# Loads of q in two parts, zeroing in smaller pieces, and two moved steps around the turn of chunk 5, in a retention and squared-ReLU kernel on one core

## The chip, the cores and the metric

The kernel runs on one core of one Trainium2 chip. Its time is the device time of one execution in microseconds (us). Before the change the median of three runs was 203.47 us (203.37, 203.47 and 203.81). A smaller number is better.

The engines are named as in the profile: PE is TensorE's matrix multiply and PEld its load of weights, DVE is VectorE, ACT is ScalarE, POOL is GpSimd, and SP is SyncE, which issues most DMAs. A suffix q (SPq, POOLq) marks work of an engine's queue, such as the issue of a DMA.

## The reference

```python
batch, n_heads, seq, head_dim = (4, 8, 768, 64)
gamma = 1.0 - 2.0 ** (-5.0 - np.arange(H))
for t in range(S):
    state = gamma[None, :, None, None] * state + einsum('bhd,bhe->bhde', k[:, :, t], v[:, :, t])
    y[:, :, t] = scale * einsum('bhd,bhde->bhe', q[:, :, t], state)
x = y.transpose(0, 2, 1, 3).reshape(3072, 512)
h = np.maximum(x @ w_in, 0.0)        # w_in: 512 x 2048
out = (h * h) @ w_out                # w_out: 2048 x 512
```

Inputs and output are float32; the output is 3072 x 512.

## The kernel before, in words

**Tiling.** The 3072 tokens are 24 chunks of 128 (six for each of the four batch entries). For a chunk the recurrence becomes matrix products: scores (k times q, masked), a state that is carried from chunk to chunk in PSUM, and outputs (values times masked scores, plus q times the state so far). The outputs of a chunk are the columns `xt` that the feed-forward part reads. That part works in blocks: block 0 has chunks 0 to 3, and each later block has two chunks. A block has a first product with `w_in`, a ReLU on ACT that moves it out of PSUM, a square on DVE, and a second product with `w_out`.

**Seven products.** For the last two chunks of block 0, and for the later blocks, the second product is not done plainly but by a scheme with seven half-size products in place of eight (in the manner of Strassen and Winograd). It needs sums of pieces of `h` made beforehand on DVE: `s1`, `s2` (`first_sums`), `s3` (`third_sums`, L1021) and `s4` (`fourth_sums`, L1025). It also needs differences of pieces of `w_out`, which `sum_w_out` (L338) makes in `w_sum`. For block 0 all this is `last_of_first` (L983). Its generator `second_products` (L1029) interleaves the plain second product of chunks 0 and 1, which collect in two PSUM tiles `ops`, with the seven products of chunks 2 and 3, in `pa`, `pb`, `pd` and `pe`. The last of the seven, which is the reader of `s4`, is kept back (`last_product`, L1091) and run inside block 1.

**Order.** Nothing is reordered by the compiler: each engine runs its instructions in the order in which the Python emits them, and waits by semaphores on the other engines. The order is written by hand. The feed-forward part is cut into numbered places, 8 for each chunk. `put(place, what, ...)` notes a step, and `before(n)` (L1370) emits all steps of place n, in the order in which they were put, between two pieces of the feed-forward part. The steps that were put by `ffn_pieces(0)`, which include the sums of `h`, are put when that generator starts, and so come last in their place. Block 0 covers the places up to 32, and block 1 begins behind place 32.

**The stretch around chunk 5.** `attend(5, None, (25, 27, 30, 32, 34))` (L1331) spreads chunk 5's steps. Place 25 has the scaling of k and the copy of v into `v_bd` on POOL (`scale_kv`, L397). Place 27 has its turn, `transpose_k` (L426): four transposes on PE into the PSUM tile `tp` and two copies on ACT (L437), one for each 64 rows of `k_bd`. Place 30 has the first half of the scores, place 32 the second half, and place 34 the outputs. `scores` (L448) has four products into the single buffer of `st` and one masking multiply on DVE (L463), which writes `pt`. The second half can start only when the mask of the first half has read `st`. `attend(6, 30, ...)` puts the two scalings of q of chunk 6 (`scale_q`, L391) at place 30, behind chunk 5's scores.

**Loads.** `load_q` (L88) brings the q of two chunks, eight heads, in one DMA of 512 KB on SP's queue, into one of two buffers. `load_kv` brings k or v of one chunk on SP. From chunk 8 on, k comes packed, by DMAs that POOL issues (`k_loads`), into `k_bigs`. The parts of `k_bigs` off the block diagonal are zeroed by POOL memsets at places 16, 34 and 43 and the ones behind them (L1341).

Of the kernel before, what the change touches and what calls it, by code (L numbers as in the profile page):

```python
# [31 lines left out]
def kernel(  # L32
# [14 lines left out]
    C = 128  # L47
# [37 lines left out]

    raw_q, raw_k, raw_v = {}, {}, {}

    def load_q(m):  # L88

        b, i = chunks[m]  # L90
        t = ldqpool.tile([P, H, 2, D], FP32, name="qn")
        src = q[b, :, i * C : (i + 2) * C, :].rearrange("h (s r) d -> s h r d", r=2)
        nc.sync.dma_start(t[:], src)
        raw_q[m] = t

    heads_of = [slice(0, H // 2), slice(H // 2, H)]
# [886 lines left out]
    def last_of_first():  # L983

        def halves_of(k, c):
            return [
                t.rearrange("e (j k) (c t) -> e k c j t", k=2, c=4)[:, k, 2 + c] for t in h2s[0]
            ]

        (a11, a12), (a21, a22) = ([halves_of(k, c) for k in range(2)] for c in range(2))  # L990
        n = NFB // 4
        s1, s2, s4 = (
            [
                t.rearrange("e (x j t) -> e x j t", x=2, t=C)[:, x]
                for x in range(2)
            ]
            for t in (spare[:, i * HN * 4 : (i + 1) * HN * 4] for i in range(3))
        )
        s3 = a21
        b = lambda k, c: lambda j: w_out_bf[j // 2][:, 2 * (j % 2) + k, c * HN : (c + 1) * HN]  # L1000
        t1, t2, t3, t4 = (lambda j, t=t: t[:, j] for t in sums)

        def add(out, in0, in1, op=ALU.add):
            nc.vector.tensor_tensor(out=out, in0=in0, in1=in1, op=op)

        def product(to, left, right, js, start=True, stop=True):
            for j in js:
                nc.tensor.matmul(  # L1008
                    to,
                    lhsT=left[j // n][:, j % n],  # L1010
                    rhs=right(j),
                    start=(start and j == 0),
                    stop=(stop and j == NFB // 2 - 1),
                    skip_group_check=True,
                )

        def first_sums(x):
            add(s1[x], a21[x], a22[x])
            add(s2[x], s1[x], a11[x], ALU.subtract)

        def third_sums():  # L1021
            for x in range(2):
                add(s3[x], a11[x], a21[x], ALU.subtract)

        def fourth_sums():  # L1025
            for x in range(2):
                add(s4[x], a12[x], s2[x], ALU.subtract)

        def second_products():  # L1029
            ops = [ps_f.tile([P, DM], FP32, name="psf") for _ in range(2)]  # L1030
            pa, pe, pd, pb = (
                t[:, n * HN : (n + 1) * HN]
                for t in [ps_f.tile([P, DM], FP32, name="psf") for _ in range(2)]
                for n in range(2)
            )
            oa, ob = (opool.tile([P, DM], FP32, name="osb") for _ in range(2))
            a, u, v = (upool.tile([P, HN], FP32, name=f"u{i}") for i in range(3))
            r0 = 2 * C

            def plain(j):  # L1040
                for f in (2 * j, 2 * j + 1):
                    for c, op in enumerate(ops):
                        nc.tensor.matmul(  # L1043
                            op[:],
                            lhsT=h_of(0, f)[:, 0, c * C : (c + 1) * C],
                            rhs=w_out_bf[f // FPQ][:, f % FPQ, :],
                            start=(f == 0),
                            stop=(f == NFB - 1),
                        )
                product(pa, a11, b(0, 0), (j,))  # L1050

            lo, hi = range(0, 4), range(4, 8)
            for j in range(4):
                plain(j)
                yield
            product(pd, s1, t1, lo)
            product(pb, s2, t2, lo, False)
            yield
            for j in range(4, 6):
                plain(j)  # L1060
                yield
            product(pe, a22, t4, lo, False)
            yield
            plain(6)
            yield
            plain(7)
            nc.scalar.activation(a[:], pa, AF.Copy)
            for c, op in enumerate(ops):
                osb = opool.tile([P, DM], FP32, name="osb")
                nc.scalar.activation(osb[:], op[:], AF.Copy)  # L1070
                nc.sync.dma_start(out[c * C : (c + 1) * C], osb[:])
            yield
            product(pd, s1, t1, hi)
            product(pb, s2, t2, hi)
            add(u[:], pb, a[:])
            yield
            product(pa, a12, b(1, 0), lo, False)
            yield
            product(pa, a12, b(1, 0), hi, False)
            nc.scalar.activation(oa[:, 0:HN], pa, AF.Copy)  # L1080
            yield
            product(pb, s3, t3, lo, False)
            yield
            product(pb, s3, t3, hi, False)
            add(v[:], pb, a[:])
            add(ob[:, HN:DM], pd, v[:])
            yield
            product(pe, a22, t4, hi)
            add(ob[:, 0:HN], pe, v[:])

            def last_product():  # L1091
                product(pd, s4, b(1, 1), range(8), False)
                add(oa[:, HN:DM], pd, u[:])
                yield
                nc.sync.dma_start(out[r0 + C : r0 + 2 * C], ob[:])
                yield
                nc.sync.dma_start(out[r0 : r0 + C], oa[:])
                yield

            kept.append(last_product())  # L1100
            yield

        return first_sums, (third_sums, fourth_sums), second_products
# [27 lines left out]
    def ffn_pieces(tb):  # L1131
        nch = BLOCKS[tb]
        TB = nch * C
        if tb == 0:
            first_sums, last_sums, second_products = last_of_first()
            put(11, first_sums, 0)
            put(17, first_sums, 1)
            put(26, last_sums[0])
            put(27, last_sums[1])
            for f in range(FPQ, NFB):  # L1140
                hp = ps_f.tile([P, TB], FP32, name="psf")
                first_product(tb, hp[:], f, slice(0, TB))
                relu(h_of(tb, f)[:, 0], hp)
                yield
            yield from second_products()
            return
        elif tb <= 2:

            for c in range(nch):
                for g in range(NQ):  # L1150
                    first_unit(tb, g, c)
                    if c * NQ + g in (1, 2, 3) and kept:
                        next(kept[0])
                    if c * NQ + g == 4:
                        kept.clear()
                    if tb in SEVEN and (c, g) == (1, 2):
                        first_sums, rest = seven_products(tb)
                        first_sums(slice(0, 4))
                    yield
            if tb in SEVEN:  # L1160
                yield from rest()
                return
        else:
            h_tiles(tb)
            per = 512 // TB
            if tb in SEVEN:
                first_sums, rest = seven_products(tb)
            for f0 in range(0, NFB, per):
                hp = ps_f.tile([P, per, TB], FP32, name="psf")
                for f in range(f0, f0 + per):  # L1170
                    first_product(tb, hp[:, f - f0, :], f, slice(0, TB))
                relu(h_of(tb, f0, f0 + per), hp, tb in SEVEN and f0 // per in (1, 3))
                if f0 // per in (1, 2, 3) and kept:
                    next(kept[0])
                if f0 // per == 4:
                    kept.clear()
                if f0 // per == 5 and tb in SEVEN:
                    first_sums(slice(0, 4))
                yield
            if tb in SEVEN:  # L1180
                yield from rest()
                return
# [102 lines left out]
    def put(place, what, *args):  # L1285
        parts.setdefault(place, []).append((what, args))
# [31 lines left out]
        put(place, load_w_out, g)  # L1318
    for m, which, place in ((4, "v", 10), (5, "k", 12), (5, "v", 14)):
        put(place, load_kv, m, which)  # L1320
    put(15, load_q, 6)
    for m, which, place in ((6, "k", 16), (6, "v", 17), (7, "k", 18), (7, "v", 19)):
        put(place, load_kv, m, which)
    put(10, cast_w, "in", 3)
# [15 lines left out]

    for j, t in enumerate(k_bigs):  # L1341
        for hh in range(2):
            put((16, 34, 43)[j] + hh, nc.gpsimd.memset, t[halves[hh], :, :, 1 - hh, :], 0.0)

    put(20, load_q, 8)
    put(41, load_q, 10)
    done = [57, 62] + [70 + 8 * j for j in range(14)]

    ahead = {
# [62 lines left out]
```

## Time and profile before

| What | Value |
|---|---|
| Median of three runs | 203.47 us |
| The profiled execution's own time | 203.39 us |
| Its span, first to last instruction | 201.6 us |
| PE busy | 195.0 us |
| DVE busy | 151.0 us |
| ACT busy | 127.1 us |
| POOL busy | 82.7 us |

The span is 1.8 us shorter than the execution's own time, which also holds what lies before the first and behind the last instruction. In rows of the timeline the first number is the start in us from the span's start, and the second is how long the row lasts. Then come the engine, the line of the kernel, the operation, what is written from what, the shape and the number of instructions put together in the row. In square brackets stands how long the engine was idle before the row and what ended that. A matmul is pipelined: the row's end is modelled and overlaps the next one, so PE's pace is read from start to start, not from the busy time.

### The profile page before, as it was taken

The page shows a single profiled execution, that of the slowest core. Times are in us where ns is not written, and L with a number is a line of the kernel's source. Part 1 is how long each engine was busy: PE and PEld are TensorE (multiplying, and loading weights), DVE is VectorE, ACT ScalarE, POOL GpSimd, SP SyncE. Part 2 cuts the span into 40 slices and gives each one's busy share as a digit, 9 for nine tenths or more (in the row PEclk, how much of TensorE's full clock was granted, in tenths as well). Part 3 has the DMA queues.
Part 4 walks back from the last instruction along what each step waited for, and adds up shares of the span by engine and source line. Part 5 has one row for each costly group of instructions (what it writes and reads, how often), then busy time and mean ns, then how long its engine had stood idle before and what let it go on. Part 6 is the DMA issues. An engine that isn't in the chain of part 4 may idle for free.

```text
span 201.6 us, 5846 instructions
## 1 busy us (share of the span) xinstructions
PE 195.0 (97%) x2362; PEld 164.6 (82%) x2362; DVE 151.0 (75%) x327; ACT 127.1 (63%) x258; POOL 82.7 (41%) x150
## 2 busy tenths in 40 slices
PE   7799999999999999999999999999999999999991
PEld 2468445779988999899999999999999999999881
DVE  3986899799598886777687697697696696484472
ACT  8864875264863666774766866864865865845710
POOL 8683760899930762154422185116362202200000
PEclk9999999999999999999999999999999999999999
DMA  5999999999987999599979399999999762101102
GB/s 166 356 375 397 343 192 196 252 201 227 305 174 182 176 163 238 172 134 180 189 152 206 114 170 221 158 242 141 192 153 140 197 94 67 66 0 52 55 0 106
DMA packets 92250, 36.02 MB, mean 179 GB/s; under 512 B 68544, under 2 KB 88256, under 8 KB 92224
## 3 DMA queue, kind: packets, MB, share of 16 engines
q1 hardware_dynamic: 73088, 31.47, 66.5%
q0 software_dynamic: 19136, 4.20, 23.3%
q8 instruction: 18, 0.29, 0.6%
q14 instruction: 8, 0.07, 0.1%
HBM read 27.26 MB, written 6.29 MB: 166 GB/s over the span
## 4 chain that ended last, share of the span: by engine, by line
PE 91%; DVE 4%; DMA 2%; issue 1%; ACT 0%; DVEq 0%
PE psf L847 42%; PE psf L884 21%; PE tp L884 7%; PE psf L1043 3%; PE psf L1008 2%; DMA qn<-in_q_dram 2%; PE y L804 2%; PE st L748 2%; PE y L797 2%; PE c_ps L775 2%; PE c_ps L653 1%; PE y L532 1%; PE st L456 1%; PE y L368 1%; DVE qs L559 1%; DVE osb L880 1%
## 5 line engine op out<-in xcount | busy, mean ns | idle before, releaser
L847 PE MATMUL psf<-xt,w_in_bf 128*128 128x256 bf16 (+2 forms) x864 | 92.3, 261 | 0.0
L847 PEld LDWEIGHTS <-w_in_bf 128*128 128x128 bf16 x864 | 70.8, 98 | 11.2
L856 ACT ACTIVATE h<-psf 128x512 bf16<-128x512 f32 x96 | 56.2, 594 | 24.3 <-PE psf L847 22.0
L726 POOL COPY v_bd<-v 64x512 bf16<-64x512 bf16 x32 | 21.7, 677 | 76.5 <-DVE v L718 75.6
L827 DVE TENSOR_TENSOR h<-h 128x512 bf16<-128x512 bf16 x80 | 32.8, 423 | 19.1 <-ACT h L856 18.4
L884 PEld LDWEIGHTS <-h 128*128 128x128 bf16 x344 | 31.7, 98 | 3.7 <-issue 0.2
L156 POOL DMA_DIRECT2D k_big<-in_k_dram x40 | 26.6, 686 | 0.1
L884 PE MATMUL psf<-w_sum,h 128*128 128x256 bf16 x168 | 23.5, 273 | 0.0
L884 PE MATMUL tp<-w_out_bf,h 128*128 128x256 bf16 x136 | 19.1, 273 | 0.0
L880 DVE TENSOR_TENSOR u<-psf,u 128x256 f32<-128x256 f32 x20 | 8.5, 424 | 12.7 <-PE psf L884 11.8
L884 PE MATMUL psf<-w_sum,k_bd 128*128 128x256 bf16 x144 | 17.9, 273 | 0.0
L880 DVE TENSOR_TENSOR osb<-psf,u 128x256 f32<-128x256 f32 x29 | 11.4, 420 | 6.6 <-PE psf L884 6.3
L884 PEld LDWEIGHTS <-k_bd 128*128 128x128 bf16 x144 | 13.8, 98 | 1.5
L784 ACT ACTIVATE s_bd<-c_ps 64x256 bf16<-64x256 f32 x29 | 10.7, 369 | 6.3 <-PE c_ps L775 6.3
L387 DVE TENSOR_TENSOR qs<-qn,qf 128x512 bf16<-128x512 f32 x20 | 13.7, 688 | 0.0
L785 ACT ACTIVATE s_bd<-c_ps 64x256 bf16<-64x256 f32 x29 | 11.0, 379 | 0.4
L755 DVE TENSOR_TENSOR pt<-st,cmask 128x512 bf16<-128x512 f32 x16 | 11.0, 687 | 0.2
L718 DVE TENSOR_TENSOR v<-stage,kf 128x512 bf16<-128x512 f32 x16 | 10.9, 683 | 0.0
L920 ACT ACTIVATE osb<-tp 128x256 f32<-128x256 f32 x8 | 3.1, 384 | 12.2 <-PE tp L884 12.2
L811 ACT ACTIVATE xt<-y 128x512 bf16<-128x512 f32 x16 | 9.6, 598 | 1.8 <-PE y L804 1.2
L825 ACT ACTIVATE h<-h 128x512 bf16<-128x512 bf16 x16 | 10.1, 630 | 0.5
L880 DVE TENSOR_TENSOR k_bd<-h 128x512 bf16<-128x512 bf16 x18 | 9.9, 553 | 0.3
(147 smaller groups left out, 290.1 us busy)
## 6 DMA issues: line engine op xcount, KB each, us to landing
qn<-in_q_dram SPq DMA_DIRECT2D x12, 512.0 KB, 5.7
out_dram<-osb SPq DMA_DIRECT2D x23, 256.0 KB, 2.6
stage<-in_v_dram SPq DMA_DIRECT2D x32, 96.0 KB, 3.9
stage<-in_moe_w_in_dram SPq DMA_DIRECT2D x4, 512.0 KB, 6.8
stage<-in_moe_w_in_dram SPq DMA_DIRECT2D x2, 1024.0 KB, 10.7
w_out_bf<-in_moe_w_out_dram POOLq DMA_DIRECT2D x4, 512.0 KB, 10.4
kn<-in_k_dram SPq DMA_DIRECT2D x6, 256.0 KB, 6.2
k_big<-in_k_dram POOLq DMA_DIRECT2D x32, 48.0 KB, 3.8
```

The lines of the kernel that those rows point to most:

```text
L156: nc.gpsimd.dma_start(t[rows, 2 * at_w : 2 * (at_w + size), p, hh, :], half_rows(k, b, 2 * p + hh, i + w, size),)
L387: engine.tensor_tensor(out=out, in0=by, in1=table[:, :, None].to_broadcast([P, H, D]), op=ALU.mult)
L718: nc.vector.tensor_tensor(out=v2.rearrange("s (u p) d -> s u p d", u=2), in0=vn, in1=kf2[:, i, :, :, None].to_broadcast([P, 2, NPAIR, D]), ...
L726: nc.gpsimd.tensor_copy(v_bd[rows, :, hh, :], v2[rows])
L755: nc.vector.tensor_tensor(out=pt[:], in0=st[:], in1=cmask2.rearrange("s r t -> s (r t)")[:, None, :].to_broadcast([P, 2 * NPAIR, C // 2]), ...
L784: nc.scalar.activation(s_bd[halves[0], :, 0, :], c[halves[0]], AF.Copy)
L785: nc.scalar.activation(s_bd[halves[1], :, 1, :], c[halves[1]], AF.Copy)
L827: nc.vector.tensor_mul(hv, hv, hv)
L847: nc.tensor.matmul(hp, lhsT=w_in_bf[g][:, cb, fq * 128 : (fq + 1) * 128], rhs=xts[tb][:, cb, cols], start=(cb == 0), stop=(cb == NCB - 1),)
L856: nc.scalar.activation(hv, hp[:], AF.Relu)
L880: nc.vector.tensor_tensor(out=out, in0=in0, in1=in1, op=op)
L884: nc.tensor.matmul(to, lhsT=left[:, j], rhs=right(j) if callable(right) else right[:, j], start=(start and j == 0), stop=(stop and j == NF ...
```

## The change

The change does five things. `load_q` can take a list of slices of heads and issues one DMA for each; the loads of chunks 6, 8 and 10 (each with its odd neighbour) are issued as two DMAs of 256 KB, at the same places as before. Each memset that zeroes a part of `k_bigs` is split in two along the chunks. The sums `s4` of block 0, two DVE instructions at place 27, become one at place 27 and one at place 30, behind all other steps there. The copy of the plain product of chunk 1 out of PSUM (ACT) and its store (a DMA on SP), which stood beside those of chunk 0, are emitted one piece later, behind the steps of places 26 and 27, and so behind chunk 5's turn.

```diff
-    def load_q(m):
+    def load_q(m, heads=(slice(0, H),)):
...
-        src = q[b, :, i * C : (i + 2) * C, :].rearrange("h (s r) d -> s h r d", r=2)
-        nc.sync.dma_start(t[:], src)
+        for part in heads:
+            src = q[b, part, i * C : (i + 2) * C, :].rearrange("h (s r) d -> s h r d", r=2)
+            nc.sync.dma_start(t[:, part], src)
...
-        def fourth_sums():
-            for x in range(2):
-                add(s4[x], a12[x], s2[x], ALU.subtract)
+        def fourth_sums(x):
+            add(s4[x], a12[x], s2[x], ALU.subtract)
...
             nc.scalar.activation(a[:], pa, AF.Copy)
-            for c, op in enumerate(ops):
+
+            def store(c):
                 osb = opool.tile([P, DM], FP32, name="osb")
-                nc.scalar.activation(osb[:], op[:], AF.Copy)
+                nc.scalar.activation(osb[:], ops[c][:], AF.Copy)
                 nc.sync.dma_start(out[c * C : (c + 1) * C], osb[:])
+
+            store(0)
             yield
             product(pd, s1, t1, hi)
             product(pb, s2, t2, hi)
             add(u[:], pb, a[:])
             yield
+            store(1)
             product(pa, a12, b(1, 0), lo, False)
...
-            put(27, last_sums[1])
+            put(27, last_sums[1], 0)
+            put(30, last_sums[1], 1)
...
-    put(15, load_q, 6)
+    put(15, load_q, 6, heads_of)
...
         for hh in range(2):
-            put((16, 34, 43)[j] + hh, nc.gpsimd.memset, t[halves[hh], :, :, 1 - hh, :], 0.0)
-
-    put(20, load_q, 8)
-    put(41, load_q, 10)
+            for to in (t[halves[hh], 0:4], t[halves[hh], 4:]):
+                put((16, 34, 43)[j] + hh, nc.gpsimd.memset, to[:, :, :, 1 - hh, :], 0.0)
+
+    put(20, load_q, 8, heads_of)
+    put(41, load_q, 10, heads_of)
```

`heads_of` is the existing pair of slices, heads 0 to 3 and heads 4 to 7 (L96).

## The prediction

> **What bounds the kernel now.** I read the page first, then the busy time by stretches, then the chain of waits from 43 to 47 us, then each engine's timeline there.
>
> ```profile
> span 201.6 us, 5846 instructions
> ...
> PE 195.0 (97%) x2362; PEld 164.6 (82%) x2362; DVE 151.0 (75%) x327; ACT 127.1 (63%) x258; POOL 82.7 (41%) x150
> ```
>
> PE is the bound. The next view shows where it is not busy; its columns are the stretch, then busy us (and instructions) of PE, PEld, DVE, ACT and POOL, the granted clock, the DMA share and GB/s.
>
> ```profile
> 43.00:47.00 4.00, 3.77 (x46) 3.17 (x44) 3.97 (x8) 2.03 (x5) 4.00 (x7) 1.00 1.48 193
> 47.00:190.00 143.00, 142.98 (x1832) 130.84 (x1830) 105.73 (x222) 95.52 (x196) 51.71 (x76) 1.00 0.90 158
> 190.00:201.60 11.60, 7.58 (x78) 6.72 (x75) 6.76 (x18) 1.91 (x4) 0.00 (x0) 1.00 0.13 46
> ```
>
> The change touches neither the start nor the end. In the middle PE idles visibly in one place, 43 to 47 us, where DVE is busy 3.97 of 4.00 us. That is chunk 5's turn and scores, and the moved steps stand there. The chain of waits goes through DVE (start, duration, what):
>
> ```profile
> 44.36 1.08 DVE h L1004 x2
> 45.45 0.61 DVE pt L463
> ```
>
> The two instructions on `h` are the sums `s4`; the mask of chunk 5's first scores stands behind them. PE's rows give the price, read from start to start:
>
> ```profile
> 38.53 0.39 PE L456 MATMUL st<-qT,k_bd 128*128 128x128 bf16 x4
> ...
> 44.00 0.60 PE L1008 MATMUL psf<-w_sum,h 128*128 128x256 bf16 x4
> 44.43 0.63 PE L456 MATMUL st<-qT,k_bd 128*128 128x128 bf16 x4
> ...
> 44.72 0.34 PE L456 MATMUL st<-qT,k_bd 128*128 128x128 bf16 x3
> 44.90 1.04 PE L1008 MATMUL psf<-w_sum,h 128*128 128x256 bf16 x8
> ...
> 46.10 0.38 PE L456 MATMUL st<-qT,k_bd 128*128 128x128 bf16 x4 [0.16 <-DVE pt L463]
> ```
>
> Four products of scores take 0.39 us for chunk 4 and 0.63 for chunk 5: 0.24 us lost, behind the first of the four. Four products of 256 columns take 44.43 - 44.00 = 0.43, so eight need 0.87; the eight at 44.90 are followed only after 1.20: another 0.33, for the mask. Together **0.57 us** can be won here, which would give 203.39 - 0.57 = 202.82. I reckon from the profiled execution's own 203.39 us, 0.08 below the median of 203.47.
>
> **The copy behind the turn.** The second of the four products needs the second copy of `k_bd`, on ACT:
>
> ```profile
> 42.90 0.39 PE L430 MATMUL tp<-ident,ks 128*128 128x128 bf16 x4
> ...
> 42.51 0.59 ACT L1070 ACTIVATE osb<-psf 128x512 f32<-128x512 f32 x1
> ...
> 43.46 1.21 ACT L437 ACTIVATE k_bd<-tp 64x512 bf16<-64x512 bf16 x2
> ...
> 47.41 0.60 ACT L856 ACTIVATE h<-psf 128x512 bf16<-128x512 f32 x1 [2.33 <-PE psf L847]
> ```
>
> The two copies end at 43.46 + 1.21 = 44.67, and PE goes on at 44.72. They started behind the copy of chunk 1's product, which now goes behind them. What is late next are the transposes: they end at 42.90 + 0.39 = 43.29, and the first output copy at 43.10. With a handover of 0.03 to 0.05 the `k_bd` copies start at 43.32 to 43.34, only 0.12 to 0.14 earlier. So 0.10 to 0.12 of the 0.24 us stays. The moved copy itself fits before ACT's idle 2.33 us. The PSUM tile that it frees is first wanted by block 1's second unit, and the ReLU of the first starts only at 47.41. Its store is one issue on SP; places 26 and 27 put nothing else on SP, and on POOL only k loads, which do not wait for it.
>
> **The sum behind the scores.** DVE around the mask:
>
> ```profile
> 44.28 0.42 DVE L1004 TENSOR_TENSOR h<-h,h 128x512 bf16<-128x512 bf16 x1
> ...
> 44.62 0.83 DVE L1004 TENSOR_TENSOR h<-h,h 128x512 bf16<-128x512 bf16 x1
> ...
> 45.37 0.68 DVE L463 TENSOR_TENSOR pt<-st,cmask 128x512 bf16<-128x512 f32 x1
> 45.97 1.28 DVE L387 TENSOR_TENSOR qs<-qn,qf 128x512 bf16<-128x512 f32 x2
> ...
> 48.29 0.68 DVE L463 TENSOR_TENSOR pt<-st,cmask 128x512 bf16<-128x512 f32 x1
> ...
> 51.82 0.43 DVE L827 TENSOR_TENSOR h<-h 128x512 bf16<-128x512 bf16 x1 [1.25 <-ACT h L856]
> ```
>
> With one sum left, DVE is free at 44.28 + 0.42 = 44.70. The scores end at 44.72 + 0.34 = 45.06, less 0.12 to 0.14: 44.92 to 44.94. So the mask waits for PE now: it runs from about 44.97 to 45.65, and PE's next scores start 0.05 later, at 45.70, where PE itself arrives at 44.77 + 0.87 = 45.64. The start moves from 46.10 to 45.68 to 45.72. **The gain is 0.38 to 0.42 us; I take 0.40**, and the sum is 203.39 - 0.40 = 202.99.
>
> Behind it DVE has the same work in another order, and three readers must still be served:
>
> ```profile
> 47.21 0.61 PE L417 MATMUL tp<-ident,qs 128*128 128x128 bf16 x8
> ...
> 48.55 1.04 PE L1008 MATMUL psf<-w_out_bf,h 128*128 128x256 bf16 x8
> ...
> 49.81 0.28 PE L532 MATMUL y<-pt,v_bd 128*128 128x128 bf16 x2
> ```
>
> All three come 0.40 earlier now. The scalings of q end 1.88 behind the mask's start (47.25 - 45.37), so at 46.85; their fifth transpose comes at 47.21 + 4 x 0.056 - 0.40 = 47.03: 0.18 to spare. The moved sum then ends at 47.2, or 47.6 if it is again stretched to 0.83; its reader, the second half of the eight at 48.55, comes at 48.6. The second mask ends at 48.9 or 49.3; its reader comes at 49.41. The last margin is 0.1, or 0.05 with the handover. DVE's idle 1.25 us before 51.82 takes up the rest.
>
> Would the stretch to 0.83 fall on the mask when the sum is gone? Durations, smallest, median and largest in ns:
>
> ```profile
> L463 DVE TENSOR_TENSOR pt<-st,cmask x8: 677/682/692, 36.8 to 62.4; 128x512 bf16<-128x512 f32 x8
> ...
> L880 DVE TENSOR_TENSOR k_bd<-h x18: 412/426/833, 72.1 to 192.6; 128x512 bf16<-128x512 bf16 x18
> ...
> 46.83 0.89 POOL L403 CAST v_bd<-vn 128x512 bf16<-128x512 f32 x1
> ...
> L403 POOL CAST v_bd<-vn x4: 616/682/886, 35.2 to 50.8; 128x512 bf16<-128x512 f32 x4
> ```
>
> DVE adds that read SBUF alone are at times stretched from 426 to 833; no mask, which reads PSUM, ever was. So hardly.
>
> **The memsets.** POOL's rows:
>
> ```profile
> L1372 POOL MEMSET k_big<- x6: 1368/1373/1800, 35.8 to 55.4; 64x1536 bf16 x4, 64x2048 bf16 x2
> ...
> 40.76 0.74 POOL L403 CAST v_bd<-vn 128x512 bf16<-128x512 f32 x1 [1.34 <-DMA vn<-in_v_dram]
> ...
> 66.19 1.39 POOL L726 COPY v_bd<-v 64x512 bf16<-64x512 bf16 x2 [8.78 <-DVE v L718]
> ...
> 61.26 0.32 PE L495 MATMUL c_ps<-v_bd,ks 128*64 128x64 bf16 x8
> ```
>
> 512 elements more cost 1.80 - 1.37 = 0.43 us, so 1536 would cost 1.28 and a fixed 0.09 is left. Six more memsets cost POOL 6 x 0.09 = 0.5 us and their gaps. The first two vanish in the 1.34 us before chunk 5's v, the last two in the 8.78; the middle two delay chunk 7's v, which stands behind them, by 0.2 us, and PE reads it only at 61.26, 5.9 us behind the start of the last memset of all (55.4). Nothing reaches PE; without that cover the price would be 0.5 us.
>
> **The q loads.** The nearest row for a load of 256 KB by four heads is the first one here (issue times in ns); then the whole load of chunk 6, issue to landing; then the range over all q loads; then SP's waits between 43 and 62 us, behind chunk 10's q and behind chunk 8's (in all, times, longest).
>
> ```profile
> L115 SPq DMA_DIRECT2D kn<-in_k_dram x3: 487/507/610, 1.3 to 2.9; - x3
> ...
> 31.65 4.50 SPq L93 DMA_DIRECT2D qn<-in_q_dram  x1
> ...
> qn<-in_q_dram SPq DMA_DIRECT2D x1, 512.0 KB, 10.5
> ...
> DMA to landing us min/median/max: 3.9/5.7/11.6
> ...
> SPq L443 <- DVE qs L387: 2.5, 1, 2.5
> SPq L1095 <- DVE osb L1004: 1.5, 1, 1.5
> ```
>
> Each second issue costs SP about 0.5 us. Chunk 6's q lands at 31.65 + 10.5 = 42.2 and is read at 45.6 after the change, so 3.4 us cover it. Those of chunks 8 and 10 are taken up by SP's waits of 1.5 and 2.5. I price all three at nothing; the ends are 0 and what the last rival below asks.
>
> **The rivals.**
>
> *More than 0.40.* If the copies of `k_bd` come early enough to hide both stalls, and the mask with them, it is the full 0.57: 202.82. Against it speaks that the transposes end at 43.29; for it, that this end is a modelled one, and that DVE, busy 3.97 of 4.00 us here, is relieved at the right point.
>
> *The moved sum blocks the second mask.* At 46.8 POOL's cast of v begins as the sum would start. If the sum must wait until the cast, alone 0.62 us, has ended at 47.45, it ends at 47.87; the second mask, which starts 1.04 behind the DVE work ahead of those steps (48.29 - 47.25), ends at 47.87 + 1.04 + 0.68 = 49.59, PE starts 0.05 later and has waited 0.23: 203.39 - 0.40 + 0.23 = 203.22. For it speaks the cast's 0.89 us beside DVE; against, that the add rows are never stretched by more than 0.41. The Trainium skill, page "SBUF — State Buffer", section "Who interferes with whom", has this mechanism: a DVE instruction with two SBUF inputs contends with a GpSimd instruction that reads SBUF, and the later one is blocked for the whole of the first. The rows here agree that such an add can be stretched, but show 0.41 at most (833 against 426).
>
> *No gain.* The mask is stretched by 0.41 after all, or DVE comes late: 203.4.
>
> *Slower.* The second half of chunk 6's q lands late. Both scalings read all heads, and on DVE the moved sum, the output sums and the second mask are queued behind them; PE waits for the scalings at 47.03. From a landing at 45.6 + 0.18 on, each us costs one; at 46.2 the gain is gone, and from 46.7 it is slower by 0.2%. If the second half, issued until about 36.7, took the longest 11.6, it would land at 48.3: 203.4 + 2.1 = 205.5. For it speaks the DMA share of 1.48 in this stretch; against, 3.4 us of room.
>
> **How the numbers follow.** Forecast 0.55, more 0.18, blocked mask 0.08, no gain 0.08, slower 0.11. About 0.2% (0.41 us) is what a measurement of this kernel can tell from no change; the bound for faster is 203.06. The forecast's 202.99 lies near it, and I give 0.40 of its 0.55 to faster, 0.15 to the same. Faster is then 0.58, same 0.31 (0.15 + 0.08 + 0.08), slower 0.11. The range 202.6 to 203.7 holds all but the slower case, with the runs' spread about 202.82 and 203.4.
>
> **What would show it.** In the changed profile: `k_bd` copies (L437 of before) starting at 43.3; the first scores 0.5 us long; the mask at 45.0 straight behind PE; the next scores at 45.7, still with a wait below 0.1; no wait at the outputs near 49; DVE idle longer before 51.4. It would be wrong if the scalings of q near 45.6 waited for a DMA, or if a stall of the old size stood at the second scores.

## The result, and the profile after

The change takes 0.3 us off the kernel.

| | before | after |
|---|---|---|
| Median | 203.44 us (203.21 to 203.81, 22 runs) | 203.10 us (203.06 to 204.13, 22 runs) |
| Ratio after / before | | 0.9981, 95% interval 0.9975 to 0.9987 |
| The profiled execution's own time | 203.39 us | 203.10 us |

Now and then one execution of several of these kernels, also of the one before, is about 1 us longer than the others; the ranges shown hold such executions too, and the medians hardly move with them.

The page of the changed kernel, and its busy time by the stretches used before (columns: stretch, then busy us and instructions of PE, PEld, DVE, ACT and POOL, the granted clock, the DMA share, GB/s):

```profile
span 201.3 us, 5858 instructions
...
PE 195.6 (97%) x2362; PEld 164.7 (82%) x2362; DVE 150.4 (75%) x327; ACT 127.2 (63%) x258; POOL 82.8 (41%) x156
```

```profile
43.00:47.00 4.00, 3.88 (x49) 3.35 (x47) 3.71 (x8) 2.14 (x5) 4.00 (x7) 1.00 1.55 198
47.00:190.00 143.00, 142.98 (x1831) 130.81 (x1828) 105.95 (x223) 95.74 (x196) 51.81 (x80) 1.00 0.89 158
190.00:201.30 11.30, 7.39 (x76) 6.54 (x73) 6.58 (x18) 1.73 (x4) 0.00 (x0) 0.95 0.13 47
```

PE's share of the span is still 97%. From 43 to 47 us it is busy 3.88 us instead of 3.77, and DVE is no longer full (3.71 instead of 3.97). The middle is as busy as before. The last stretch is shorter by 0.3 us, but that takes in what the middle won, since everything behind it comes earlier. PE's rows around chunk 5's scores separate the two:

```profile
44.42 0.49 PE L457 MATMUL st<-qT,k_bd 128*128 128x128 bf16 x4
44.75 1.31 PE L1009 MATMUL psf<-w_sum,h 128*128 128x256 bf16 x8
45.90 0.39 PE L457 MATMUL st<-qT,k_bd 128*128 128x128 bf16 x4
...
49.23 0.22 PE L525 MATMUL y<-qT,s_bd 128*128 128x128 bf16 x1
...
196.78 0.61 PE L885 MATMUL tp<-w_out_bf,v_bd 128*128 128x128 bf16 x8
```

The last of these rows started at 196.97 before:

```profile
196.97 0.61 PE L884 MATMUL tp<-w_out_bf,v_bd 128*128 128x128 bf16 x8
```

The first scores take 0.49 us instead of 0.63. The second scores start at 45.90 instead of 46.10, and this 0.20 arrives at PE's last products as 0.19 (the granted clock of 0.95 in the last stretch costs nothing that shows there: from these products to the issue of the last stores, at 197.64 before and 197.45 now, it is 0.67 us in both). The profiled execution is shorter by 0.29 us, so 0.10 us is won **behind** PE's last product.

The stall at the second scores is not gone either. Four products take 0.43, as the prediction read, so the eight that start at 44.75 should be done with at 45.62; PE went on at 45.90. The chain of waits of the changed kernel says what came between (start, duration, what):

```profile
43.31 0.59 ACT k_bd L438
...
44.54 0.20 ACT osb L1071
...
45.04 0.39 ACT osb L1084
45.42 0.04 issue
45.47 0.60 PE psf L1009 x4
```

DVE has left the chain, and ACT stands in it: the moved copy of chunk 1 (L1071), then the copy of `pa` into the output tile (L1084), and only then the last four of PE's eight products. The mask itself came when it was forecast, behind PE and not behind DVE's other work:

```profile
44.28 0.42 DVE L1005 TENSOR_TENSOR h<-h,h 128x512 bf16<-128x512 bf16 x1
44.95 0.69 DVE L464 TENSOR_TENSOR pt<-st,cmask 128x512 bf16<-128x512 f32 x1 [0.26 <-PE st L457]
...
46.76 0.42 DVE L1005 TENSOR_TENSOR h<-h,h 128x512 bf16<-128x512 bf16 x1
```

So two questions were open: why the forecast 0.40 us became 0.20, and where the 0.10 us behind the last product comes from.

### The profile page after: what moved, and what is told of

The parts are those of the page before. It is cut to its first block, busy times and chain, and to the rows that moved or that the text cites. A ratio compares the mean times of both kernels' runs of the same rounds, so it can differ in the third digit from the quotient of the medians.

```text
span 201.3 us, 5858 instructions
## 1 busy us (share of the span) xinstructions
PE 195.6 (97%) x2362; PEld 164.7 (82%) x2362; DVE 150.4 (75%) x327; ACT 127.2 (63%) x258; POOL 82.8 (41%) x156
## 4 chain that ended last, share of the span: by engine, by line
PE 91%; DVE 3%; DMA 2%; ACT 1%; issue 1%; DVEq 0%
PE psf L848 42%; PE psf L885 21%; PE tp L885 7%; PE psf L1043 3%; PE psf L1009 2%; DMA qn<-in_q_dram 2%; PE y L805 2%; PE st L749 2%; PE y L798 2%; PE c_ps L776 2%; PE c_ps L654 1%; PE y L533 1%; PE st L457 1%; PE y L369 1%; DVE qs L560 1%
```

## The experiments

In each run the kernel before was executed beside it on the same chip; its medians there were 203.39, 203.39 and 203.41 us.

**The sum alone.** Only the second `s4` is moved.

```diff
...
-            put(27, last_sums[1])
+            put(27, last_sums[1], 0)
+            put(30, last_sums[1], 1)
```

> Only the second sum s4 moves from place 27 to 30; copies, loads and memsets as before. Theory A (PE's two waits at chunk 5's scores are all that counts): the wait for the second k_bd copy stays (scores 0.63 us long), the mask starts straight behind PE at 45.10 instead of 45.37, the second scores start at 45.82 instead of 46.10, so 0.27 us less in the profile, and no wait of the product into pe, since the copy of pa still ends at 45.08. Rival B (the loads or memsets bring the gain): about 0, within 0.1 us of before. Theory C (the kernel before has runs of about 203.4 and of about 203.7 because DVE's work ahead of the mask is stretched once more in some of them): with the sum gone DVE has 0.3 us of room there, so no runs near 203.7; rival: they stay, in about 4 of 10.

Measured: 203.47 us (203.14 to 204.33, 11 runs), ratio 1.0005 (0.9994 to 1.0015). Nothing is won in the end, and rows of PE, DVE and POOL show where it went:

```profile
45.84 0.38 PE L456 MATMUL st<-qT,k_bd 128*128 128x128 bf16 x4
...
48.64 0.82 PE L1008 MATMUL psf<-w_out_bf,h 128*128 128x256 bf16 x6 [0.18 <-DVE osb L1004]
```

```profile
46.91 0.89 DVE L1004 TENSOR_TENSOR h<-h,h 128x512 bf16<-128x512 bf16 x1
...
48.17 0.75 DVE L1004 TENSOR_TENSOR osb<-psf,u 128x256 f32<-128x256 f32 x2
```

```profile
46.80 0.70 POOL L403 CAST v_bd<-vn 128x512 bf16<-128x512 f32 x1
```

The second scores start 0.26 us earlier than before (45.84 against 46.10). But the moved sum now starts at 46.91, behind the start of POOL's cast of v, and takes 0.89 instead of 0.42. The output sums on `psf` behind it are late, and the last of the seven products, which started at 48.55 before, starts at 48.64. It collects in `pd`, which the first of the two output sums must have read. It was to come 0.26 earlier and comes 0.09 later, so 0.35 us are given back. This is the prediction's rival of the blocked sum, with another victim: not the second mask, but the reader of `pd`. In the whole change the same sum starts at 46.76, ahead of the cast at 46.82, and takes 0.42.

**The copy alone.** Only the copy and store of chunk 1 go behind the turn (`store(0)` stays where it was, and `store(1)` stands behind the next piece, as in the change).

> Only the copy and store of chunk 1's product go behind chunk 5's turn; both sums s4 stay at place 27. Theory A: the k_bd copies start at 43.31 instead of 43.46 and the first scores are done 0.14 us sooner, but the copy of pa now ends at 45.42 instead of 45.08, the product into pe waits for it until 45.47 (before 45.34), and the mask still ends at 46.05 behind the two sums: second scores at 46.10, 0.0 us gained. Rival (the copy carries the gain): 0.14 us or more less. Theory C: runs near 203.7 remain.

Measured: 203.38 us (203.36 to 204.56, 11 runs), ratio 0.9998 (0.9979 to 1.0016). PE's first scores get shorter as in the whole change, but the second scores start where they did before, since both sums still stand ahead of the mask. PE's wait within the eight products (1.31 us for their row) is there already, hidden by the wait for the mask:

```profile
44.44 0.49 PE L456 MATMUL st<-qT,k_bd 128*128 128x128 bf16 x4
44.77 1.31 PE L1008 MATMUL psf<-w_sum,h 128*128 128x256 bf16 x8
46.10 0.38 PE L456 MATMUL st<-qT,k_bd 128*128 128x128 bf16 x4
```

**Loads and memsets alone**, with both moves left out.

> Only the loads of q in halves and the split memsets. Theory A: nothing, within 0.05 us of before in the profile, second scores at 46.10. Rival B: 0.1 to 0.3 us less, with DVE's sums (0.83 us for the second before) no longer stretched. Rival: more, up to 0.5 us, if SP's extra issues delay chunk 5's v. Theory C: runs near 203.7 remain.

Measured: 203.26 us (202.99 to 203.64, 11 runs), ratio 0.9988 (0.9975 to 1.0002).

**The copy later still.** The whole change, but chunk 1's copy stands behind the copy of `pa`, so that ACT does that one first. Its edit against the changed kernel:

```diff
             yield
-            store(1)
             product(pa, a12, b(1, 0), lo, False)
             yield
             product(pa, a12, b(1, 0), hi, False)
             nc.scalar.activation(oa[:, 0:HN], pa, AF.Copy)
+            store(1)
             yield
```

> The whole change, but the copy and store of chunk 1's product go one step further, behind the copy of pa (the first half of the output tile oa). Theory A (the change gave back 0.28 us because the product into pe waits for the copy of pa, which the moved copy delays): the copy of pa ends at about 44.95, the wait of 0.28 us is gone, the second scores wait for the mask only and start at 45.68 to 45.72 instead of 45.90, so 0.2 us less than the changed kernel and 0.4 less than before: about 202.9. Rival (another wait stands right behind, the mask or the scalings of q, and takes it): 203.0 to 203.1.

Measured: 202.94 us (202.90 to 204.43, 11 runs), ratio 0.9985 (0.9971 to 1.0). PE, ACT and DVE:

```profile
44.76 1.04 PE L1009 MATMUL psf<-w_sum,h 128*128 128x256 bf16 x8
45.75 0.38 PE L457 MATMUL st<-qT,k_bd 128*128 128x128 bf16 x4
```

```profile
44.55 0.38 ACT L1083 ACTIVATE osb<-psf 128x256 f32<-128x256 f32 x1
44.83 0.59 ACT L1071 ACTIVATE osb<-psf 128x512 f32<-128x512 f32 x1
```

```profile
44.27 0.83 DVE L1005 TENSOR_TENSOR h<-h,h 128x512 bf16<-128x512 bf16 x1
45.02 0.68 DVE L464 TENSOR_TENSOR pt<-st,cmask 128x512 bf16<-128x512 f32 x1
```

The eight products run without a break again (1.04 us for the row instead of 1.31), and the second scores start at 45.75 instead of 45.90. What made PE wait is thereby shown. The last four of the eight are `product(pe, a22, t4, hi)`. `pe` and `pa` are the two halves of one PSUM tile, and the product into `pe` waits until ACT has read `pa`. In the changed kernel that copy ended at 45.04 + 0.38 = 45.42, PE was ready at 44.75 + 0.43 = 45.18, and went on at 45.47. The Trainium skill, page "PSUM — Partial Sum Buffer", section "PSUM bank collisions raise a hardware error", says that two engines must not be in one bank of the same partitions at the same time, even at different columns, and that semaphores should guard a bank and not an address. The trace agrees as far as it goes: the product into one half waited 0.28 us for the copy of the other half. Before the change the copy of `pa` was early enough to be seen nowhere:

```profile
44.69 0.38 ACT L1080 ACTIVATE osb<-psf 128x256 f32<-128x256 f32 x1
```

It ended at 45.07, and PE came to the last four at 44.90 + 0.43 = 45.33.

**Both moves, no loads and no memsets.**

> Sum and copy moved as in the change, loads and memsets as before. Theory A: PE's places as in the changed kernel (first scores 0.49 us, product into pe at 45.47, second scores at 45.90, 0.20 less than before), and what the changed kernel gained beyond that lies behind the last matmul and comes with the loads or memsets: here the stretch from the last matmul to the end is 4.24 us as before, not 4.13, so 203.2. The runs near 203.7 are gone, as in the changed kernel, since the product into pe waits for ACT whether a DVE sum is stretched or not. Rival (the whole gain is the two moves): 203.1.

Measured: 203.25 us (203.19 to 203.47, 11 runs), ratio 0.9995 (0.9987 to 1.0004). The second scores start as in the whole change:

```profile
45.90 0.39 PE L456 MATMUL st<-qT,k_bd 128*128 128x128 bf16 x4
```

So the moves are worth the 0.20 us at PE in the profiled executions (203.19 against 203.39), and what the change gains beyond that belongs to the loads and memsets. The executions alone don't show the 0.20: they spread from 203.19 to 203.47, for which no profile here has the cause, and the interval holds 1.

**The q loads alone, and the memsets alone.**

> Only the loads of q in halves. Theory D (the end is 0.11 us shorter because three more DMAs shift the last stores to other completion semaphores, which SP waits for in a fixed order at the end): 0.11 us less behind the last matmul, 4.13 us, so 203.26 as with the loads and memsets together. Rival (six more POOL instructions shorten POOL's last drain): 4.24, so 203.38.

> Only the split memsets. Theory D: nothing, 203.38, the end 4.24 us behind the last matmul. Rival: 203.26 and 4.13.

Measured: the loads 203.69 us (203.47 to 204.11, 11 runs), ratio 1.0020 (1.0011 to 1.0029); the memsets 203.00 us (202.69 to 203.35, 11 runs), ratio 0.9987 (0.9978 to 0.9996). Both expectations fell. The two edits are not free: one costs, the other pays, and neither does it near the instructions that it edits. The issue of the last two stores (the row) against the end of the span (the line above it), first with the q loads alone, then with the memsets alone:

```profile
core 0 of [0], span 202.0 us
...
197.67 0.82 SPq L979 DMA_DIRECT2D out_dram<-osb  x2
```

```profile
core 0 of [0], span 200.9 us
...
197.40 0.83 SPq L978 DMA_DIRECT2D out_dram<-osb  x2
```

From this issue to the end of the span it is 4.3 us with the loads and 3.5 with the memsets. The kernel before has it here, and the changed kernel below it:

```profile
197.64 0.84 SPq L978 DMA_DIRECT2D out_dram<-osb  x2
```

```profile
197.45 0.83 SPq L979 DMA_DIRECT2D out_dram<-osb  x2
```

With their spans of 201.6 and 201.3 that is 4.0 and 3.9 us. The spans are rounded. With each profiled execution's own time in place of the span, which adds the same 1.8 us to all, it is:

| Kernels | Own time less the start of the last stores |
|---|---|
| Neither edit (before, sum alone, copy alone, both moves) | 5.75, 5.74, 5.75, 5.74 us |
| Both edits (after, loads and memsets alone, copy later, sum at 31) | 5.65, 5.64, 5.64, 5.61 us |
| q loads only | 6.09 us |
| Memsets only (memsets alone, its three further executions, moves and memsets) | 5.32, 5.36, 5.33, 5.33, 5.37 us |

In these fourteen profiles it goes with the two edits; each group lies within 0.05 us. It is about +0.34 us for the loads, -0.41 for the memsets and -0.11 for both. What differs there is seen in the closing instructions, which the profile books on the `with` line around the kernel. They are waits and drains of the engines' queues; a row has their number, the smallest, median and largest duration in ns, and the first and last start. Before, and with the memsets alone:

```profile
L1407 POOLq DRAIN  x2: 40/141/242, 200.9 to 201.3; - x2
```

```profile
L1408 POOLq DRAIN  x2: 40/66/93, 200.4 to 200.7; - x2
```

Wherever the memsets are split, POOL's long drain takes 93 to 102 ns instead of 236 to 242. Another row goes with the memsets too: the fetches of instructions (queue q14: packets, MB, share of the DMA engines) from 197.5 us on, behind the last stores. Before, and with the memsets alone:

```profile
q14 instruction: 2, 0.02, 1.0%
```

```profile
q14 instruction: 1, 0.01, 0.6%
```

All five profiles with whole memsets have two such fetches there, the second at the very end (201.6 us in the kernel before). All nine with split memsets have one there, and have another at 168.5 to 169.7 us that the five lack. So six more instructions on POOL go with a fetch at another time. That this fetch makes the end longer or shorter was not tried.

The waits of SP's queue near the end (in all, times, longest) show both edits, the loads alone against the memsets alone:

```profile
SPq L1408 <- DMA out_dram<-osb: 1.2, 3, 0.6
SPq L1408 <- PEq L1408: 1.1, 2, 0.9
```

```profile
SPq L1408 <- DMA out_dram<-osb: 0.9, 3, 0.4
SPq L1408 <- PEq L1408: 0.6, 2, 0.5
```

With split loads SP's waits for the output DMAs add up to 1.2 us, with whole loads to 0.9; the wait put down to PE's queue is 1.1 us with whole memsets and 0.6 to 0.7 with split ones. Each holds in all fourteen profiles. Three more DMAs on SP shift which completion semaphores the last three stores use (101, 103 and 104 with the split loads, 107, 109 and 110 before), and SP passes its closing waits in a fixed order, so more of them come behind the last landing. That the shift causes the longer end was not tried by itself.

**The second sum one place later.** As the later copy, and the moved sum at place 31, so that it can't meet the cast of v.

```diff
-            put(30, last_sums[1], 1)
+            put(31, last_sums[1], 1)
```

> As the kernel with the copy one step later, but the second sum s4 at place 31, behind the sum that forms v and the first one into the output tile. Theory E (the moved sum, when POOL's cast of chunk 6's v gets ahead of it, is stretched by 0.4 to 0.5 us and with it the output sum behind it, whose reading of pd the last product waits for): the second sum no longer meets the cast, no wait before the last product at 48.2, second scores at 45.7, and none of the slower runs (203.2 to 203.3) that the kernel with the later copy had in 3 of 11: 202.9 in all but stray ones. Rival (those runs have another cause): they stay, and the median is the same within 0.05.

Measured: 202.95 us (202.86 to 204.11, 11 runs), ratio 0.9983 (0.9971 to 0.9994). The sum stands between the output sums now, takes 0.41 us, and the second scores stay where the later copy has them:

```profile
47.64 0.41 DVE L1005 TENSOR_TENSOR h<-h,h 128x512 bf16<-128x512 bf16 x1
```

```profile
45.78 0.38 PE L457 MATMUL st<-qT,k_bd 128*128 128x128 bf16 x4
```

The median is that of place 30. With the sum at place 30, 3 of the 11 runs lay at 203.21 to 203.31; at place 31 all but the longest lay within 202.86 to 202.99. That fits a sum that no longer meets the cast, but no profile caught one of the three, and 11 runs each are too few to show it.

**Moves and memsets.** As the last, with q loaded whole (`put(15, load_q, 6)` and so on, without `heads_of`).

> The copy one step later (behind the copy of pa), the second sum s4 at place 31, the split memsets, and q in whole loads. Theory D, now by engine: behind the last landing the closing sequence takes 1.37 us with the memsets split, 2.10 with the q loads split, 1.63 with both, 1.79 with neither. So against the kernel with both (202.95) the end is 0.26 us shorter, and the middle is as there (second scores at 45.7 to 45.8): 202.7. Rival (the end belongs to the placement of each single program and does not add up): 202.9 to 203.1.

Measured: **202.65 us** (202.57 to 203.86, 6 runs), ratio 0.9958 (0.9945 to 0.9972). It is below the kernel before, and its median is also below the changed kernel's 203.10, which was not executed beside it. Its profiled execution was the one at 203.86, so no row in the middle of it is read.

**The memsets alone, executed three times more.** The profile of the memsets alone had shown the second scores at 45.85 although nothing was moved there, and its execution took 202.72, less than the median. The same kernel again:

> The split memsets alone again, for its profile: this kernel had runs near 202.7, 203.0 and 203.3, and its profile was one near 202.7, with neither sum s4 stretched and second scores at 45.85. Theory C: a run near 203.0 has one of the two sums at 0.83 instead of 0.42 us and second scores at 46.1; a run near 203.3 has one more DVE instruction ahead of the mask stretched and second scores at 46.4 or later. Rival: the second scores stand at the same place and the difference lies in the end.

> As for the first look at this kernel: near 202.7 no sum s4 stretched, near 203.0 one, near 203.3 one more DVE instruction ahead of the mask, if theory C holds.

> As for the first look at this kernel: near 202.7 no sum s4 stretched, near 203.0 one, near 203.3 one more DVE instruction ahead of the mask, if theory C holds.

Measured: 202.99, 202.95 and 202.98 us. DVE's sums and PE's second scores in the earlier execution of 202.72, then in the first of the three:

```profile
44.28 0.75 DVE L1004 TENSOR_TENSOR h<-h,h 128x512 bf16<-128x512 bf16 x2
```

```profile
45.85 0.38 PE L456 MATMUL st<-qT,k_bd 128*128 128x128 bf16 x4
```

```profile
44.27 1.17 DVE L1004 TENSOR_TENSOR h<-h,h 128x512 bf16<-128x512 bf16 x2
```

```profile
46.09 0.38 PE L456 MATMUL st<-qT,k_bd 128*128 128x128 bf16 x4 [0.16 <-DVE pt L463]
```

In one execution neither sum is stretched, in the others one of the two is, by 0.42 us, and PE's second scores and the execution's time differ from the earlier ones by 0.22 to 0.27. So the same program has this difference from run to run. The profile of the loads and memsets alone, at 202.99 against a median of 203.26, was also one without a stretched sum. The runs of the kernel before at about 203.15 beside those at 203.39 would fit this; no profile of it caught one. If so, the moves win their 0.20 us against the more frequent kind of execution, and little or nothing against the other, in which the second scores would start near 45.85 without them.

## Why the prediction was right, and where its steps were not

The time was forecast at 203.0 us and is 203.10. Two errors of opposite sign lie in it: the moves gave 0.20 us less than forecast, and an end that was priced at nothing gave 0.11. That the total came so near is therefore in part luck. The prediction gave 0.40 of its chances to a gain beyond its bound of 0.2% and 0.15 to one within it; the ratio of 0.9981 is 0.19%, just within, with the bound inside its interval.

- **The bound.** Right: PE, with its one visible idle place from 43 to 47 us.
- **The copy behind the turn.** Right: the `k_bd` copies start at 43.31, where 43.32 to 43.34 was forecast, and 44.75 - 44.42 = 0.33 us to the next product is 0.11 over chunk 4's pace, where 0.10 to 0.12 was forecast to stay.
- **The sum behind the scores.** The mask was right (44.97 to 45.65 forecast, 44.95 to 45.64 measured). The step "PE's next scores start 0.05 later, at 45.70, where PE itself arrives at 44.77 + 0.87 = 45.64" failed: PE arrived at 45.90. The 0.87 took the eight products to be free of waits, since before they waited for nothing. But the prediction followed the moved ACT copy only forward to the ReLU at 47.41 and to the PSUM tile that it frees. It did not ask which ACT instruction the copy was put ahead of: the copy of `pa`, whose PSUM tile PE needs next. That made a new wait of 0.28, and the sum's gain was 0.05 (from 44.90 to 46.10 it was 1.20, from 44.75 to 45.90 it is 1.15). With the copy behind that of `pa`, the start is 45.75, 0.05 behind the forecast, with one sum stretched ahead of the mask.
- **The readers behind.** In the changed kernel all three were served, and no wait stands ahead of the outputs at 49.23. The second mask ended at 48.22 + 0.68 = 48.90, where 48.9 was forecast without a stretch. That the moved sum was not stretched hung on 0.06 us, between its start at 46.76 and the cast's at 46.82; with the sum alone this was lost, and the rival of the blocked sum came true with another victim than the mask. The stretch there was 0.47 us (0.89 against 0.42), more than the 0.41 that the prediction's rows had shown at most: the sum ended at 46.91 + 0.89 = 47.80, and it would have been 47.92 had it waited for the whole cast (46.80 + 0.70, and 0.42 behind it). That the last product also waits for the output sum that reads `pd` was not in the prediction.
- **A stretched mask.** Right: no mask was stretched in any profile shown here.
- **Memsets and loads.** That nothing reaches PE was right. "The change touches neither the start nor the end" was wrong: the end is longer by 0.34 for the loads and shorter by 0.41 for the memsets. The fixed price of a memset was set too high: two halves take 1.40 to 1.41 us at 47.59 and 49.31 where the whole took 1.37, so about 0.04 and not 0.09 for each memset more, which changes nothing here. "Each second issue costs SP about 0.5 us" held for chunk 10 (1.17 in place of 0.62) but not for chunk 6, whose two issues take 6.99 in place of 4.50:

```profile
32.12 6.99 SPq L94 DMA_DIRECT2D qn<-in_q_dram  x2
```

  They ended at 39.11, where the last rival had the second half issued by 36.7.
- **The slower rival.** Chunk 6's q was in time all the same; DVE's scalings start at 45.56 without a wait:

```profile
45.56 1.28 DVE L388 TENSOR_TENSOR qs<-qn,qf 128x512 bf16<-128x512 f32 x2
```

The parts add up, read from single profiled executions. From the 203.39 of before, the moves give 203.19 (203.19 in the profiled execution of the moves alone), with the loads and memsets 203.08 (203.10 measured). The later copy gives 203.39 - 0.35 - 0.11 = 202.93 (202.94 measured), and without the split loads 203.39 - 0.35 - 0.41 = 202.63 (202.65 measured).

## What to carry to other kernels

When an instruction is moved within an engine's order, look not only at who waits for it, but at each instruction that it is now ahead of, and at who waits for that one; halves of a PSUM tile count as one buffer there. Two moves that win nothing each can win something together, since what the one leaves in place (here the sums ahead of the mask, or the later start at which the cast is met) takes back what the other wins: undo them one at a time before you judge either. And when a change adds DMAs or instructions to a queue, compare the time behind the last store too, however far from the edit it lies.

## What the runs showed of the hardware

- **DVE adds beside POOL.** An add of two SBUF operands (128x512 bf16) takes 0.42 us, and at times 0.83 to 0.89. One such stretch lies beside POOL's cast of v, as the Trainium skill, page "SBUF — State Buffer", section "Who interferes with whom", would have it: a DVE instruction with two SBUF inputs contends with a GpSimd instruction that reads SBUF. But the `s4` sums at 44.3 to 44.6 were stretched while POOL did nothing but issue loads of k, as its row in the first further execution of the memsets shows:

```profile
41.42 5.46 POOL L156 DMA_DIRECT2D k_big<-in_k_dram  x8
```

  By the section of the Trainium skill an add should not meet that work, for it infers that making such a load's descriptors needs the write interface, of which an add takes none. The measurement shows a stretch of 0.4 us there in nine of the fourteen profiles and none in the other five, and which of two adds is hit changes from run to run. Most adds beside such issues are not stretched, and no run takes the issues away, so the cause stays open.
- **The end of the program.** From the issue of the same last stores to the end of the span it is 3.5 to 4.3 us, by how many DMAs and POOL instructions came long before. With six more memsets POOL's closing drain is shorter by about 0.15 us and the end by 0.41. What lies behind the rest of that was not tried. The Trainium skill, page "Runtime: NRT & Kernel Launch", section "Instruction fetch mechanics", says that an engine's instructions are fetched in blocks of 256 and that crossing into a new one is mostly hidden. A crossing that is not hidden would fit a gap that comes and goes with an engine's count of instructions. The traces have a fetch that moves from 168.5 us to the very end where the memsets are whole, but not that POOL waited for it, and it does not explain the 0.34 of the loads.
- **Still open:** some runs of the kernel before lie at 203.67 to 203.80 us, and some of the memsets alone at 203.2 to 203.35; no profile caught one.
